# Attention and two gated feed-forward layers on one core: how heads and weights are loaded at the start, and which tiles hold layer 1's last sums

## The chip, the core and the metric

The kernel runs on one core of a Trainium2 chip. The metric is the device time in microseconds of one execution, the median of several. Engines are named as the profile names them: PE (TensorE matmul), PEld (its weight loads), DVE (VectorE), ACT (ScalarE), POOL (GpSimd), SP (SyncE, which here only issues DMAs).

## What is computed

Attention over 4 batches of 8 heads, sequence 576, head size 64, with a causal mask and a forget-gate bias made of running sums of `s`. The result, 2304 tokens by 512, goes through two feed-forward layers of width 2048, the first with a hard-swish gate, the second with Silu.

```
cum  = cumsum(maximum(s, 0)); bias = -(cum[:, None] - cum[None, :])
p    = softmax(where(causal, -1e9, q @ k.T / 8 + minimum(bias, 0)))
x    = concat_heads(p @ v)                      # 2304 x 512
h    = x @ w1_in;  x2 = (h * clip(h + 3, 0, 6) / 6) @ w1_out
h    = x2 @ w2_in; out = (h * sigmoid(h)) @ w2_out
```

The scale is a factor of `q`, `k` and `v` are float32, and the four weight matrices are float64 in memory.

## The kernel before

**Numbers.** Each product is three matmuls (high by high, low by high, high by low), so that operands are held in a high and a low part. A weight matrix is cut into 16 pieces, `i0` to `i15` of w_in and `o0` to `o15` of w_out, each a DMA of 512 KB of raw 32-bit word pairs. A piece of layer 1 is made usable by six operations after its load (class `Chunk`, line 147 on): ACT `fields` (L159, L160), DVE `join` (L168, L172, L175), ACT `high` (a cast at L120), DVE `low` (L186). That is four DVE operations a piece, 128 for the 32 pieces of layer 1. The class `Feed` steps all pieces through these stages, one stage of each of several pieces with every call of `tick`: three ticks at the start, then 0.4 a slot over the first nine slots, then 2 a slot.

**Stages.** Nine slots of attention heads alone come first, in which PE is kept from idling by small matmuls (`keep_clock`, L86). Then come slots that hold one head and one step of layer 1: `first` (the product with a w_in piece, L259 to L261), the gate (ACT L271, DVE L272), `second` (the product with a w_out piece, L298 to L300). A step needs the pieces `i` and `o` of its number. The steps run over two blocks of tokens in turn: block 0 with pieces 0 to 7, block 1 with pieces 0 to 7 two at a time, then block 0 and block 1 with pieces 8 to 15. The gates are counted here as g0 to g7 (block 0), g8 to g11 (block 1, pairs), g12 and on. Layer 2 starts where the last sums of layer 1 are complete, with matmuls at L1008 to L1010 and L1024 to L1026, a gate on ACT (L1066, L1067) and DVE (L1068).

**Order.** The tile framework's scheduler sets the order of each engine's instructions at build time from its own estimates of time; on the chip each engine runs its list in order, and an instruction that waits holds all that stand behind it in that list. So does a DMA that waits in SP's list.

**Start.** `s` is loaded, made non-negative and summed by one scan over 576 elements (L343, L346) into `crow`. Each of the first 14 heads has a tile of its own (`inA...`) with q and k of 64 rows, and two more rows of sums (L418, L419: DMAs out of `crow`) and of constants (L406, L407: memsets on POOL); v comes by a third DMA (L396). The tiles borrow the slots of pieces not loaded yet (`spare`). The first three raw weight loads (L147) stand in SP's list between the first two heads' loads and their rows of sums. `cum_d` is a copy of the sums in DRAM, out of which later heads take theirs.

**Border of the layers.** `finish1` (L698 on) takes the last block's sums out of PSUM into four tiles `o7_*` by ACT and DVE copies, in the slot `s4` of `w7pool` and in slots `mag` of the stage pool, which are those in which raw words become magnitudes (ACT L160). They are stored by L712 to `x2T_d` and read back. A first use of Silu at L1066 brings a load of ACT's function table. `outs2` asks for a tick of layer 2's w_out pieces in the last steps of layer 1 (L1127 on).

## Time and profile before

| | us |
|---|---|
| median of 3 runs | 1021.71 (1020.31 to 1023.79) |
| profiled execution, its own time | 1023.73 |
| span of its trace | 1021.6 |
| PE busy | 991.8 (97%) |
| DVE busy | 723.7 (71%) |
| ACT busy | 523.4 (51%) |
| POOL busy | 204.5 (20%) |

The page gives PE 97% of the span. Its 40 slices of 25.5 us show where the rest is: PE has 8, 8, 7, 8 tenths in the first four slices, 9 in all others but one (8, at 638 to 664 us) and the last (7). The granted clock is under full only in the first four slices. DMA moves 153 to 297 GB/s in those slices and 44 to 70 in the next five. The chain that ended last is 89% PE.

### The profile page before, as it was taken

What the parts mean: (1) busy time and instruction counts of PE and PEld (TensorE: products, weight loads), DVE (VectorE), ACT (ScalarE), POOL (GpSimd) and SP (SyncE); (2) the same over time, 40 slices, a digit from 0 to 9 for tenths busy, and PEclk for the clock granted to TensorE, in tenths of its full rate; (3) what the DMA queues carried; (4) which work ended last, traced back from release to release, by engine and by line L of the source; (5) the groups of instructions that cost most, each with busy time, mean ns of one, the idle gap of its engine ahead of it and who ended that gap; (6) DMA issues with size and microseconds to landing.
All of it is one profiled execution on the core that took longest, in us unless ns stands there. A gap on an engine that the chain in (4) does not pass through costs nothing.

```text
span 1021.6 us, 18386 instructions
## 1 busy us (share of the span) xinstructions
PE 991.8 (97%) x6404; PEld 914.1 (89%) x6404; DVE 723.7 (71%) x1788; ACT 523.4 (51%) x1143; POOL 204.5 (20%) x382
## 2 busy tenths in 40 slices
PE   8878999999999999999999999899999999999997
PEld 5777999999999999999998888789988899888996
DVE  6799987788778888887738896977574343743343
ACT  6688755554555665665516563755353232532232
POOL 5001133444344444444411221000000000000000
PEclk9989999999999999999999999999999999999999
DMA  4685122222312222222114956343354332433411
GB/s 153 209 297 182 44 61 70 61 64 56 93 51 73 78 71 71 78 72 70 58 43 145 373 224 226 120 178 132 127 187 162 136 140 77 173 135 115 144 72 63
DMA packets 52068, 124.80 MB, mean 122 GB/s; under 512 B 10004, under 2 KB 31752, under 8 KB 48648
## 3 DMA queue, kind: packets, MB, share of 16 engines
q1 hardware_dynamic: 51528, 122.97, 35.7%
q8 instruction: 51, 0.84, 0.3%
q10 hardware_dynamic: 448, 0.66, 0.2%
q14 instruction: 41, 0.34, 0.1%
HBM read 98.96 MB, written 24.63 MB: 121 GB/s over the span
## 4 chain that ended last, share of the span: by engine, by line
PE 89%; DVE 5%; DMA 2%; ACT 2%; POOL 1%; issue 1%; SPq 0%; DVEq 0%; ACTq 0%; POOLq 0%
PE ph L259 6%; PE ph L260 6%; PE acc L299 6%; PE ph L261 6%; PE acc L300 6%; PE acc L298 6%; PE a L1024 6%; PE a L1025 6%; PE a L1026 6%; PE h L1008 5%; PE h L1009 5%; PE h L1010 5%; PE poB L616 4%; PE pt0B L566 1%; PE pt1B L566 1%; PE poA L631 1%
## 5 line engine op out<-in xcount | busy, mean ns | idle before, releaser
L299 PE MATMUL acc<-gl,wo 128*128 128x256 f32 (+1 forms) x512 | 153.8, 301 | 2.8 <-DVE gl L279 2.8
L259 PE MATMUL ph<-xh,wi 128*128 128x256 f32 (+1 forms) x512 | 153.3, 300 | 0.3 <-DVE g L272 0.3
L300 PE MATMUL acc<-gh,wo 128*128 128x256 f32 (+1 forms) x512 | 152.5, 299 | 0.0
L260 PE MATMUL ph<-xl,wi 128*128 128x256 f32 (+1 forms) x512 | 152.4, 298 | 0.0
L261 PE MATMUL ph<-xh,wi 128*128 128x256 f32 (+1 forms) x512 | 151.9, 297 | 0.0
L298 PE MATMUL acc<-gh,wo 128*128 128x256 f32 (+1 forms) x512 | 146.5, 301 | 0.1
L1066 ACT ACTIVATE gh<-h 128x384 fp32r<-128x384 f32 x96 | 50.3, 524 | 180.7 <-DVE h L1074 180.3
L1024 PE MATMUL a<-wo,gh 128*128 128x512 f32 x288 | 113.8, 395 | 2.4 <-ACT gh L1066 2.4
L1025 PE MATMUL a<-wo,gh 128*128 128x512 f32 x288 | 113.7, 395 | 0.0
L299 PEld LDWEIGHTS acc<-gl,wo 128*128 128x128 f32 x512 | 97.5, 191 | 6.9 <-DVE gl L279 3.6
L259 PEld LDWEIGHTS ph<-xh,wi 128*128 128x128 f32 x512 | 98.0, 191 | 4.2 <-DVE g L272 0.8
L300 PEld LDWEIGHTS acc<-gh,wo 128*128 128x128 f32 x512 | 97.5, 190 | 3.7
L260 PEld LDWEIGHTS ph<-xl,wi 128*128 128x128 f32 x512 | 97.9, 191 | 2.9
L261 PEld LDWEIGHTS ph<-xh,wi 128*128 128x128 f32 x512 | 97.8, 191 | 2.9
L298 PEld LDWEIGHTS acc<-gh,wo 128*128 128x128 f32 x512 | 96.5, 190 | 4.2 <-DVE gh L122 0.3
L1026 PE MATMUL a<-wo,gl 128*128 128x512 f32 x288 | 89.6, 393 | 1.2 <-DVE gl L1068 1.2
L1068 DVE TENSOR_TENSOR gl<-h,gh 128x384 fp32r<-128x384 f32 x96 | 53.4, 556 | 40.7 <-ACT h L1067 38.8
L1074 DVE TENSOR_TENSOR h<-h,u 128x384 f32<-128x384 f32 x72 | 40.0, 556 | 54.0 <-PE h L1010 53.7
L271 ACT ACTIVATE g<-ph,half 128x512 f32<-128x512 f32 (+1 forms) x76 | 50.3, 664 | 54.1 <-PE ph L261 53.4
L114 POOL TENSOR_SCALAR gh<-g 128x512 fp32r<-128x512 f32 x68 | 50.1, 737 | 133.2 <-DVE g L272 125.5
L272 DVE SCALAR_TENSOR_TENSOR g<-g,ph 128x512 f32<-128x512 f32 (+1 forms) x76 | 49.7, 655 | 33.4 <-ACT g L271 33.1
L1008 PE MATMUL h<-x0t,w 128*128 128x384 f32 x192 | 65.3, 340 | 0.7 <-DVE u L1074 0.7
(231 smaller groups left out, 2552.9 us busy)
## 6 DMA issues: line engine op xcount, KB each, us to landing
w<-w_d SPq DMA_DIRECT2D x18, 1792.0 KB
w_d<-w SPq DMA_DIRECT2D x8, 1792.0 KB
k2B<-in_kT_dram SPq DMA_DIRECT2D x64, 144.0 KB
rawi<-in_w1i_dram SPq DMA_DIRECT2D x16, 512.0 KB
rawo<-in_w1o_dram SPq DMA_DIRECT2D x16, 512.0 KB
rawi<-in_w2i_dram SPq DMA_DIRECT2D x16, 512.0 KB
rawo<-in_w2o_dram SPq DMA_DIRECT2D x16, 512.0 KB
q2B<-in_qT_dram SPq DMA_DIRECT2D x64, 80.0 KB
```

Of the source, the lines that this page charges most:

```text
L259: nc.tensor.matmul(o, wih[:, cs], xh[c], start=c == 0, stop=False)
L260: nc.tensor.matmul(o, wih[:, cs], xl[c], start=False, stop=False)
L261: nc.tensor.matmul(o, wil[:, cs], xh[c], start=False, stop=c == NDC - 1)
L298: nc.tensor.matmul(a, woh[:, cs], gh[:, jj, :], start=b0, stop=False)
L299: nc.tensor.matmul(a, woh[:, cs], gl[:, jj, :], start=False, stop=False)
L300: nc.tensor.matmul(a, wol[:, cs], gh[:, jj, :], start=False, stop=b1)
L1008: nc.tensor.matmul(ps, w[:, 0, cs], xh[:, c, :], start=c == 0, stop=False)
L1009: nc.tensor.matmul(ps, w[:, 0, cs], xl[:, c, :], start=False, stop=False)
L1024: nc.tensor.matmul(accs[t], gh[:, k, cs], woh, start=b0, stop=False)
L1025: nc.tensor.matmul(accs[t], gh[:, k, cs], wol, start=False, stop=False)
L1026: nc.tensor.matmul(accs[t], gl[:, k, cs], woh, start=False, stop=b1)
L1068: nc.vector.tensor_tensor(out=gl[:, i, o], in0=g, in1=f32(gh[:, i, o]), op=ALU.subtract)
```

## The change

- `keep_clock` at the start issues 18 matmuls, before 34.
- The first 14 heads are loaded in pairs (`load_two`): q, k, v and the rows of sums of two heads are one DMA each, and the constants of two heads one memset each. For the first pair, k, v and the second head's rows of sums are issued from ACT's queue, and its rows come out of `crow`; all later heads take theirs from `cum_d`. Eleven slots are borrowed rather than fourteen.
- The scan of `s` is done in two parts, 256 and 320 elements.
- A raw weight load of layer 1 is preceded by a copy of one element by POOL into the tile it will fill. The source is the end of `crow` for the first three, and from the fifth piece on the joined word of the piece four before it. The load can therefore not be issued before that piece's `join`. The three first loads come after the rows of sums and the store of `cum_d`.
- `split_rows` comes one slot later, and its rows borrow other slots.
- In the last block `finish1` uses tiles of the weight pool (slots `i0`, `i1`, in which layer 2's pieces `i8`, `i9` will be loaded) in place of `s4` and `mag`.
- A Silu of one element (`warm`) is put ahead of the last block's steps.
- `outs2` asks for more ticks in the last steps of layer 1: `min(2u + 2, t - 1)` for `u = t - 8`, before `u + 1`.

```
@@ -88,7 +88,7 @@
     def heads_of(x):
         return x.bitcast(BF16).rearrange("p (n two) -> p n two", two=2)[:, :, 1]
 
-    keep_clock(34, busy[:, :512])
+    keep_clock(18, busy[:, :512])
 
     NZ = (NFULL - 1) * P
     cmask = cpool.tile([P, NZ + P], F32, tag="cmask", name="cmask")
...
@@ -138,13 +138,15 @@
             pool, tag = self.home
             return pool.tile(shape, dt, tag=tag, name=f"{name}{self.nm}")
 
-        def load(self):
+        def load(self, queue=nc.sync, after=None):
             if self.src.dtype == F32:
                 self.val = self.place([P, DM], F32, "raw")
-                nc.sync.dma_start(self.val, self.src)
+                queue.dma_start(self.val, self.src)
             else:
                 raw = self.place([P, 2 * DM], I32, "raw")
-                nc.sync.dma_start(raw, self.src.bitcast(I32))
+                if after is not None:
+                    pool_copy(f32(raw[:1, :1]), after)
+                queue.dma_start(raw, self.src.bitcast(I32))
                 words = raw.rearrange("p (n two) -> p n two", two=2)
                 self.words = words[:, :, 0], words[:, :, 1]
 
...
@@ -211,7 +213,9 @@
             if lo == "v":
                 self.ch[t - 2].low(lo)
             if self.t < n:
-                self.ch[self.t].load()
+                if self.ch[self.t].key[1] == 0 and self.t >= 4:
+                    after = self.ch[self.t - 4].val[:1, :1]
+                self.ch[self.t].load(queue, after)
             self.t += 1
 
 
...
@@ -337,13 +341,17 @@
 
 
     srow, crow = [
-        wpool.tile([BH, S], F32, tag=f"{kd}{NF // 2 - 1}", name=f"{kd}row") for kd in "io"
+        wpool.tile([BH, S], F32, tag=f"{kd}{NF - 2}", name=f"{kd}row") for kd in "io"
     ]
     nc.sync.dma_start(srow, s)
-    nc.vector.tensor_scalar(
-        out=srow, in0=srow, scalar1=0.0, scalar2=1.0 / SCALE, op0=ALU.max, op1=ALU.mult
-    )
-    nc.vector.tensor_tensor_scan(crow, srow, srow, 0.0, ALU.add, ALU.bypass)
+    for a, z in ((0, T1), (T1, S)):
+        sr, cr = srow[:, a:z], crow[:, a:z]
+        nc.vector.tensor_scalar(
+            out=sr, in0=sr, scalar1=0.0, scalar2=1.0 / SCALE, op0=ALU.max, op1=ALU.mult
+        )
+        nc.vector.tensor_tensor_scan(
+            cr, sr, sr, crow[:, a - 1 : a] if a else 0.0, ALU.add, ALU.bypass
+        )
 
     def split_rows():
 
...
@@ -352,7 +360,7 @@
 
         f = NF - 1
         hi, lo = row(f"i{f}", "cumh"), row(f"o{f}", "cuml")
-        one, neg = row(f"i{NF // 2 - 2}", "one"), row(f"o{NF // 2 - 2}", "neg")
+        one, neg = row(f"o{NF - 3}", "one"), row(f"i{NF - 2}", "neg")
         nc.gpsimd.memset(f32(one), 1.0)
         nc.gpsimd.memset(f32(neg), -1.0)
         nc.scalar.copy(hi, crow)
...
@@ -389,16 +397,35 @@
             b, h, nm, nk, nq = self.b, self.h, self.nm, self.nk, self.nq
             if self.at < 14:
 
-                t = wpool.tile([P, 2 * DM], F32, tag=spare[self.at], name=f"in{nm}")
-                self.q2, self.k2 = t[:, :nq], t[:, nq : nq + nk]
-                self.va = t[:, DM + nk :][:, : self.nkc * D].rearrange("p (c d) -> p c d", d=D)
-                self.load_qk()
-                nc.sync.dma_start(self.va, v1[b, h, :, : self.nkc, :])
+                i = self.at % 2
+                if i == 0:
+                    self.load_two()
+                self.q2, self.k2, self.va = [x[:, i] for x in two[self.at // 2]]
                 return
             tags = ("qs", "kl") if self.whole and self.slot else ("q2", "k2")
             self.q2 = apool.tile([P, nq], F32, tag=tags[0], name=f"q2{nm}")
             self.k2 = apool.tile([P, nk], F32, tag=tags[1], name=f"k2{nm}")
             self.load_qk()
+
+        def load_two(self):
+            b, h, nm, nk, kc = self.b, self.h, self.nm, self.nk, self.nkc
+            j = self.at // 2
+            qk = wpool.tile([P, 2, 2, nk], F32, tag=spare[3 * (j // 2) + 2 * (j % 2)], name=f"in{nm}")
+            if j % 2 == 0:
+                two["v"] = wpool.tile([P, 4, kc, D], F32, tag=spare[3 * (j // 2) + 1], name=f"inv{nm}")
+            va = two["v"][:, 2 * (j % 2) :][:, :2]
+            q2, k2 = qk[:, 0], qk[:, 1]
+            two[self.at // 2] = q2, k2, va
+            nc.gpsimd.memset(q2[D : D + 2], 1.0)
+            nc.gpsimd.memset(k2[D : D + 2], -1.0)
+            hs = slice(h, h + 2)
+            nc.sync.dma_start(q2[:D], qT[b, hs, :, :nk].rearrange("h d n -> d h n"))
+            (nc.sync if self.at else nc.scalar).dma_start(
+                k2[:D], kT[b, hs, :, :nk].rearrange("h d n -> d h n")
+            )
+            (nc.sync if self.at else nc.scalar).dma_start(
+                va, v1[b, hs, :, :kc, :].rearrange("h p c d -> p h c d")
+            )
 
         def load_qk(self):
             b, h, nk = self.b, self.h, self.nk
...
@@ -413,8 +440,21 @@
 
 
             nk, q0, bh = self.nk, self.q0, self.bh
+            if self.at < 14:
+                if self.at % 2 == 0:
+                    q2, k2, _ = two[self.at // 2]
+                    if self.at:
+                        rows = cum_d[bh : bh + 2, :nk].rearrange("(o h) n -> o h n", o=1)
+                        nc.sync.dma_start(k2[D : D + 1], rows)
+                        nc.sync.dma_start(q2[D + 1 : D + 2], rows)
+                    else:
+                        for i in range(2):
+                            queue = (nc.sync, nc.scalar)[i]
+                            queue.dma_start(k2[D : D + 1, i], crow[i : i + 1, :nk])
+                            queue.dma_start(q2[D + 1 : D + 2, i], crow[i : i + 1, :nk])
+                return
             if self.whole:
-                src = crow if self.at < 4 else cum_d
+                src = cum_d
                 nc.sync.dma_start(self.k2[D : D + 1, :], src[bh : bh + 1, :nk])
                 nc.sync.dma_start(self.q2[D + 1 : D + 2, :], src[bh : bh + 1, q0:nk])
                 return
...
@@ -698,8 +738,12 @@
         n = sizes[blk][1]
         per = 512 // n
         for i, c in enumerate(range(0, NDC, per)):
-            pool, tag = (gpool, "g") if blk < NB1 - 1 else (stage, "mag") if i else (w7pool, "s4")
-            o = pool.tile([P, per, n], F32, tag=tag, name=f"o{blk}_{c}")
+            if blk < NB1 - 1:
+                o = gpool.tile([P, per, n], F32, tag="g", name=f"o{blk}_{c}")
+            else:
+                if i % 2 == 0:
+                    both = wpool.tile([P, 2, n], F32, tag=f"i{i // 2}", name=f"o{blk}_{c}")
+                o = both[:, i % 2 :][:, :1, :]
             a = sums1.pop((blk, c))
             if (blk, c) in kept:
                 for k in range(per):
...
@@ -811,10 +855,11 @@
     loaded = 2
     for hd in heads[:loaded]:
         hd.load()
-    ticks(3)
     for hd in heads[:loaded]:
         hd.load_cum()
     nc.sync.dma_start(cum_d, crow)
+    for _ in range(3):
+        feed.tick(after=crow[:1, S - 1 :])
     heads[0].places()
     k = 0
     p1 = p2 = None
...
@@ -838,7 +883,7 @@
                 tk[i] = int(feed_at)
                 feed_at -= tk[i]
         slot(cur, p1, p2, nx, loads, has_step, tk)
-        if nslot == 2:
+        if nslot == 3:
             split_rows()
         p1, p2 = cur, p1
         nslot += 1
...
@@ -1109,6 +1154,8 @@
         c0.enter_context(tc.tile_pool(name="ps_acc2", bufs=2, space=PSUM, reuse_waits="tile"))
     ]
     z0 = step
+    warm = stage.tile([P, DM], I32, tag="mag", name="warm")
+    nc.scalar.activation(f32(warm)[:, :1], f32(xsplit[NB1 - 1][0][0][NDC - 1][:, T1 : T1 + 1]), AF.Silu)
     while step < len(flat):
         t = step - z0
         first(step, 0)
...
@@ -1127,7 +1174,7 @@
         second(step - 1, 1)
         step += 1
         if t >= NF // 2:
-            outs2(t - NF // 2 + 1)
+            outs2(min(2 * (t - NF // 2) + 2, t - 1))
     second(step - 1, 0)
     second(step - 1, 1)
     c0.close()
```

**Pace of the conversions.** Of the 128 DVE conversion operations of layer 1, the order has this many ahead of each gate's L272:

| ahead of | g0 | g1 | g4 | g7 | g8 | g11 | g13 |
|---|---|---|---|---|---|---|---|
| before | 24 | 29 | 54 | 82 | 99 | 120 | 128 |
| after | 50 | 59 | 80 | 102 | 111 | 128 | 128 |

Ahead of the first score reduction (L523 on `pb0A0_0`) there are 6 before and none after. Between it and g8 four more rows of L523 stand after than before.

**The start, in SP's list.** `inA0_0` and `inA0_1` are the first heads' tiles (after: `inA0_0` and `inA0_2` are those of the first two pairs), `orow` is the tile of the sums. Before:

```order
L396 DMA inA0_0_160<-in_v1_dram 128x128
L409 DMA inA0_1_166<-in_qT_dram 64x256
L410 DMA inA0_1_166<-in_kT_dram 64x256
L396 DMA inA0_1_166<-in_v1_dram 128x128
L147 DMA rawi0_0_172<-in_w1i_dram 128x1024
L147 DMA rawo0_0_174<-in_w1o_dram 128x1024
L147 DMA rawi0_1_176<-in_w1i_dram 128x1024
L418 DMA inA0_0_160<-orow_156 1x16x16
L419 DMA inA0_0_160<-orow_156 1x16x16
L418 DMA inA0_1_166<-orow_156 1x16x16
```

After:

```order
L422 DMA inA0_0_146<-in_qT_dram 64x2x256
L422 DMA inA0_2_178<-in_qT_dram 64x2x256
L454 DMA inA0_0_146<-orow_140 1x16x16
L453 DMA inA0_0_146<-orow_140 1x16x16
L860 DMA cum_d_119<-orow_140 32x576
L423 DMA inA0_2_178<-in_kT_dram 64x2x256
L426 DMA invA0_0_147<-in_v1_dram 128x2x128
L448 DMA inA0_2_178<-cum_d_119 1x2x256
L449 DMA inA0_2_178<-cum_d_119 1x2x256
L422 DMA inA0_4_239<-in_qT_dram 64x2x256
L149 DMA rawi0_0_158<-in_w1i_dram 128x1024
L149 DMA rawo0_0_161<-in_w1o_dram 128x1024
```

The three raw loads moved from ahead of the rows of sums to behind them, behind the store of `cum_d`, and behind two reads from it.

**Up to the first gate, in DVE's list.** The rows just ahead of g0 (L272 on `g0`), where `rawX`, `magX` and `wX` are a piece's tiles, with layer and number. Before:

```order
L523 ISA pb0A1_2_654,mxA1_2_653<-ps0A1_2_664,cmask_120 128x128
L523 ISA mxA1_2_653 128x1
L523 ISA pb1A1_2_655,mxA1_2_653<-ps1A1_2_667,cmask_120 128x256
L523 ISA mxA1_2_653 128x1
L544 RECIPROCAL sums1_129<-sums1_129 128x2
L186 TENSOR_TENSOR wo0_2_764<-mago0_2_673,wo0_2_764 128x512
L272 SCALAR_TENSOR_TENSOR g0_627<-g0_627,ph0_607 128x256
```

After:

```order
L583 TENSOR_SCALAR sums0_111<-sums0_111 128x2
L678 TENSOR_TENSOR xtA1_0_612<-poA1_1_700,sums1_113 128x2x64
L170 SCALAR_TENSOR_TENSOR rawo0_6_853<-rawo0_6_853 128x512
L188 TENSOR_TENSOR wi0_5_937<-magi0_5_846,wi0_5_937 128x512
L174 TENSOR_SCALAR magi0_6_939<-magi0_6_939 128x512
L584 RECIPROCAL sums0_111<-sums0_111 128x2
L276 SCALAR_TENSOR_TENSOR g0_584<-g0_584,ph0_564 128x256
```

The piece being converted there is number 2 before and numbers 5 and 6 after.

**The border, in ACT's list.** `p1_0_0` is the first copy that layer 2 makes; `gh20_0` is the first gate on Silu. Before:

```order
L1083 COPY p1_0_0_9296<-h2_1_9297 128x384
L160 ACTIVATE mago1_5_9375<-rawo1_5_9133 128x512
L160 ACTIVATE mago1_6_9386<-rawo1_6_9176 128x512
L160 ACTIVATE mago1_7_9397<-rawo1_7_9219 128x512
L120 CAST wo1_5_9395<-mago1_5_9375 128x512
L1066 ACT_TABLE_LOAD
L1066 ACTIVATE gh20_0_9294<-h11_0_0_9321 128x384
```

After:

```order
L1128 COPY p1_0_0_9329<-h2_1_9330 128x384
L161 ACTIVATE rawo1_15_9666<-rawo1_15_9666 128x512
L120 CAST wo1_10_9657<-mago1_10_9247 128x512
L120 CAST wo1_11_9812<-mago1_11_9648 128x512
L161 ACTIVATE rawi1_8_9668<-rawi1_8_9668 128x512
L162 ACTIVATE magi1_8_9672<-rawi1_8_9668 128x512
L120 CAST wo1_12_9821<-mago1_12_9659 128x512
L1111 ACTIVATE gh20_0_9327<-h11_0_0_9354 128x384
```

The table load is gone from ahead of the gate, and so are three magnitudes and a cast; three casts and the fields of `rawo1_15` and `rawi1_8` stand there now.

**The border, in SP's list.** The stores of the last sums and the loads behind them. Before:

```order
L712 DMA x2T_d_137<-o7_0_9233 128x512
L712 DMA x2T_d_137<-o7_2_9239 128x512
L712 DMA x2T_d_137<-o7_1_9236 128x512
L712 DMA x2T_d_137<-o7_3_9242 128x512
L147 DMA rawo1_15_9699<-in_w2o_dram 128x1024
```

After:

```order
L756 DMA x2T_d_121<-o7_0_9268 128x512
L149 DMA rawo1_15_9666<-in_w2o_dram 128x1024
L756 DMA x2T_d_121<-o7_2_9273 128x512
L756 DMA x2T_d_121<-o7_0_9268 128x512
L756 DMA x2T_d_121<-o7_2_9273 128x512
L149 DMA rawi1_8_9668<-in_w2i_dram 128x1024
L149 DMA rawi1_9_9670<-in_w2i_dram 128x1024
```

`rawi1_8` and `rawi1_9` go into slots that the `o7` tiles hold, so that they can't be issued before these stores have landed.

## Rows read from the trace of the kernel before

**Rows 1.** Busy time of each engine in five stretches: length, busy (count), clock, DMA share, GB/s

```profile
12.79:46.98 34.19, 29.96 (x197) 23.25 (x195) 24.93 (x101) 22.94 (x70) 1.25 (x5) 0.95 0.57 166
46.98:108.29 61.31, 50.07 (x331) 45.56 (x330) 59.16 (x173) 51.14 (x121) 4.43 (x14) 0.89 0.66 223
108.29:128.00 19.71, 19.08 (x162) 18.83 (x163) 19.47 (x52) 14.90 (x36) 2.68 (x5) 1.00 0.18 49
200.00:300.00 100.00, 100.00 (x847) 99.53 (x846) 81.11 (x243) 51.82 (x134) 37.97 (x71) 1.00 0.24 68
640.00:660.00 20.00, 16.55 (x69) 13.53 (x69) 19.64 (x40) 15.73 (x30) 0.00 (x0) 0.91 0.37 122
```

**Rows 2.** PE timeline at the start: start us, us, line, out<-in, count, idle before

```profile
1.45 8.99 PE L86 MATMUL idle<-busy 128*128 128x512 bf16 x34 [1.45 <-DVE half L101]
11.73 0.46 PE L504 MATMUL ps0A<-inA 66*128 66x128 f32 x2 [1.29 <-POOL inA L407]
```

**Rows 3.** GpSimd timeline at the start

```profile
3.63 1.15 POOL L96 TENSOR_SCALAR_AFFINE_SELECT cmask<-cmask 128x128 f32<-128x128 f32 x1
4.84 0.30 POOL L407 MEMSET inA<- 2x256 f32 x1
```

**Rows 4.** SP queue timeline at the start: issue time and length of DMA instructions

```profile
0.73 0.40 SPq L342 DMA_DIRECT2D irow<-in_s_dram  x1
...
8.24 0.59 SPq L419 DMA_DIRECT2D inA<-orow  x1
```

**Rows 5.** DVE timeline at the start

```profile
2.68 0.63 DVE L343 TENSOR_SCALAR irow<-irow 32x576 f32<-32x576 f32 x1 [1.28 <-DMA irow<-in_s_dram]
...
12.79 0.28 DVE L523 CUSTOM_DVE_ANT_0 pb0A<-ps0A,cmask 128x128 f32<-128x128 f32 x1
```

**Rows 6.** PE timeline at the border of the layers

```profile
631.68 0.34 PE L1008 MATMUL h<-x0b,w 128*128 128x384 f32 x1
...
640.37 0.50 PE L1024 MATMUL a<-wo,gh 128*128 128x512 f32 x1 [0.19 <-ACT gh L1066]
...
643.22 0.97 PE L1026 MATMUL a<-wo,gl 128*128 128x512 f32 x3 [1.20 <-DVE gl L1068]
646.25 0.79 PE L1024 MATMUL a<-wo,gh 128*128 128x512 f32 x1 [2.06 <-ACT gh L1066]
```

**Rows 7.** DVE timeline inside the stretch of conversions

```profile
50.30 0.69 DVE L168 SCALAR_TENSOR_TENSOR rawo<-rawo 128x512 int32<-128x512 int32 x1
50.90 0.42 DVE L172 TENSOR_SCALAR mago<-mago 128x512 int32<-128x512 int32 x1
51.24 0.41 DVE L272 SCALAR_TENSOR_TENSOR g<-g,ph 128x256 f32<-128x256 f32 x1
...
52.11 0.69 DVE L175 CUSTOM_DVE_ANT_0 mago<-rawo,mago 128x1024 uint16<-128x1024 uint16 x1
52.72 0.68 DVE L186 TENSOR_TENSOR wi<-magi,wi 128x512 fp32r<-128x512 f32 x1
53.32 0.42 DVE L523 CUSTOM_DVE_ANT_0 pb1A<-ps1A,cmask 128x256 f32<-128x256 f32 x1
```

**Rows 8.** SP and ACT timelines: an uncontended weight load issued, and its first ACT operation

```profile
619.74 0.33 SPq L147 DMA_DIRECT2D rawo<-in_w2o_dram  x1
623.10 0.66 ACT L159 ACTIVATE rawo<-rawo 128x512 int32<-128x512 uint32 x1 [0.80 <-DMA rawo<-in_w2o_dram]
```

**Rows 9.** Chain of waits, two stretches: start us, us, what

```profile
63.48 4.99 DMA rawo<-in_w1o_dram
...
631.84 3.98 DMA x2T_d<-o
```

**Rows 10.** ACT timeline, before and at the border of the layers

```profile
546.30 0.69 ACT L271 ACTIVATE g<-ph,half 128x512 f32<-128x512 f32 x1 [4.21 <-PE ph L261]
...
638.49 1.28 ACT L1066 ACT_TABLE_LOAD   x1
639.79 0.53 ACT L1066 ACTIVATE gh<-h 128x384 fp32r<-128x384 f32 x1
```

98 lines of the change are left out of this document (72 added, 26 removed).

## The prediction

> **What bounds the kernel now.** I read the busy times by stretch first, because the shares of the whole span hide what matters here [rows 1]. Cut at the first score reduction (12.79), g0 (46.98) and g8 (108.29), they show two kernels. From g8 on PE is the bound: busy 19.08 of 19.71 us in the next stretch, and all of 100 us further on. Before g8 it is DVE: 59.16 of 61.31 us between g0 and g8, while PE has 50.07 at a clock of 0.89. So up to g8 the time is DVE's work plus its idle time, and an edit that moves work on PE, ACT or SP counts only if DVE gets its inputs sooner or later. Then I read the start. PE does dummies until 10.44 and its first score starts at 11.73 [rows 2]. Its row puts the wait down to POOL's memset, but that ended at 5.14 [rows 3]; the last of the rows of sums is issued at 8.24 [rows 4], so it is those DMAs that PE waits for. DVE reduces that score at 12.79 [rows 5]. The third place is the border of the layers: of 640 to 660 us PE is busy 16.55 at 0.91 [rows 1], after three waits of 0.19, 1.20 and 2.06 us, 3.45 together, on ACT and DVE [rows 6]. The clock's share there is about 0.09 x 16.55 = 1.5 us.
>
> **The start: earlier by about 3.9 us.** Without the raw loads in front, what decides is POOL's list. Its affine mask starts at 3.63 and takes 1.15, the memset behind it starts at 4.84 and takes 0.30 for 256 elements [rows 3]. With 512 elements in each of the two memsets around it I estimate the end of the second at 5.4 us. The row of sums goes into partitions that this memset writes, so its DMA starts then. The price of such a small DMA lies between 1.95 us (the load of `s`: issued at 0.73, its reader starts at 2.68) [rows 4, 5] and 3.5 us (8.24 to 11.73, with the raw loads in the same engines) [rows 2, 4]. I take one a little over 2 us, since the raw loads are gone from there: first score at 7.8, and with the 1.06 us of before between score and reduction [rows 2, 5], DVE starts at 8.9. The 18 dummies (8.99 / 34 = 0.26 each) end near 6.2, which leaves PE a gap of 1.6 us where it now has 1.29, so I put the smaller `keep_clock` at nothing. The halved scan is hidden under the memsets likewise.
>
> **DVE up to g8: longer by about 10 us of work, shorter in idle time.** From 12.79 to 108.29 DVE is busy 24.93 + 59.16 = 84.1 us of 95.5, idle 11.4, of which 9.3 lie ahead of g0 and 2.15 behind it [rows 1]. The order puts 111 conversion operations ahead of g8 where 99 stood, and it no longer does 6 of them ahead of the first score: 18 more in this stretch. Start to start, L168 takes 0.60, L172 0.34, L175 0.61 and L186 0.60 [rows 7], 0.54 on average, so 18 x 0.54 = 9.7 us. Four more rows of score reduction are at most 4 x 0.28 [rows 5]; I take 0.6. The work is 84.1 + 9.7 + 0.6 = 94.4, and g8 falls at 8.9 + 94.4 + idle = 103.3 + idle. It is level with before at an idle time of 5.0 us.
>
> No row shows how much idle time the new order has. Its lower bound is the 2.15 us of before behind g0, where conversions already stand between all other work; its upper bound is the 11.4 us of before. I take 6.1: the 26 conversions put ahead of g0 stand in the part that was idle, and this part will look more like the stretch behind g0, whose row it is nearest to (2.15); but raw words can't come before the rows of sums, the store of `cum_d` and its reads are through, and the first reductions will still wait for PE and ACT, some 4 us. That gives g8 at 109.4, **+1.1 us**, with ends of -2.8 and +6.4.
>
> **The tie of the loads.** A raw load now waits for POOL's copy, which waits for the join four pieces back, and later loads and copies of both lists wait behind it: SP's reads for the next heads, POOL's memsets for them. The chain from such a join to the first operation of the new piece is the copy and the issue (some 0.5), the landing, and 0.6 of ACT. The landing takes 3.36 us with free DMA engines (619.74 to 623.10) [rows 8] and 4.99 in the loaded start [rows 9]. So the chain is 4.5 to 6.1 us. In the new order, between such a join and the first DVE operation of the piece four later, stand operations that I sum by their kinds to 4.9 to 6.6 us. At the nearer landing, 3.36 to 4, the tie costs nothing, for that DVE work covers it; at 4.99 the shorter ones lack up to 1.2 us. I take nothing, since the same tie spreads out the burst in which the 4.99 arose.
>
> **Behind g8.** Conversions that stood here have been done, 12 of the 29 left before. PE idles 0.63 us in this stretch [rows 1]; the rest of the work is unchanged. I take **-0.6 us** (ends -0.6 and 0).
>
> **The border.** All times here are from B = 631.68, layer 2's first matmul [rows 6]. The table load of 1.28 us [rows 10] leaves ACT's list ahead of the gate, and it goes where ACT idles over 4 us at a time (4.21 ahead of 546.30) [rows 10]; without that cover it would cost those 1.28. What is late next is not the table. The stores of the last sums take until about B + 4.1 (631.84 + 3.98) [rows 9]. Now `rawi1_8` waits in SP's list for them, is issued near B + 4.6 and lands 3.36 to 4.99 later, at B + 8.0 to 9.6. ACT's list has its fields, its magnitude and a cast (about 0.6 each, as the magnitudes and casts there) ahead of the first gate, which so starts at about B + 9.8, where it now starts at B + 8.1 (639.79) [rows 10]. PE, out of first products at B + 8.5, waits near 2 us where it waited 0.19. But its later waits shrink, as they wait for the same chain of ACT and DVE: the last one ended at B + 14.57 (646.25) [rows 6]. I put it at B + 15 to 15.7, so **+0.9 us**. Ends: -0.7, where the DMA lands at its best and the casts are taken in the gaps, and +2.5, with 4.99 us for it and the 5 us of conversions that the faster `outs2` puts on DVE there.
>
> The first gate on Silu starts 1.30 us after its table load does [rows 10], so the row shows no time behind the load. The Trainium skill ("ScalarE: Activation LUTs", section "What ACT_TABLE_LOAD costs") counts a drain of 1380 ns beside the 1283 ns, 2.66 us in all. By that the border would give back 1.38 us more and the sum below would be 0.0 instead of +1.4. The trace doesn't bear it out, and I go by the row.
>
> **The sum.** +1.1 - 0.6 + 0.9 = +1.4 us: 1025.1 against the profiled execution's own 1023.73 us (its span is 1021.6, the 2.1 around it don't change). The median of the runs is 2.0 lower, 1021.71, so **1023.1 us**. All ends at once give -4.1 and +8.9. A difference under 0.3%, 3.1 us, is about what a measurement of this kernel can't tell from no change.
>
> **Rivals.**
> Faster: the conversions really fill the idle time. DVE's idle falls to 2.15 us from the first reduction on, g8 comes 2.8 us earlier, -0.6 follows. At the border the new tiles free the raw slots and the three waits shrink to between none and all: -0.7 to -4.95 (3.45 + 1.5). That is -4.1 to -8.4, about -6: 1015.7 us. For it: the 9.3 idle us ahead of g0 are real, and conversions are the only work at hand that needs no PE. Against it: both must come out well, and ACT's list puts a late load ahead of the first gate.
> Slower: the tie is too short. It decides from the point where a landing takes over 4.1 us or so: then most of the first 28 pieces come late, 24 of them under the tie, in pairs, and DVE waits about 0.7 us for each pair, with SP's and POOL's lists held meanwhile. 12 x 0.7 = 8.4 us on top of my sum less what idle of 6.1 already holds (about 2): 1023.1 + 6.4 = 1029.5. For it: the 4.99 row, and DMA engines 0.66 busy from g0 to g8 [rows 1, 9]. Against it: fewer loads are out at a time.
> The change doesn't do what it says at the start: POOL or the pair's larger loads hold the first score at 11 us or later. The 3 us or so don't come off: 1026. For it: the loads of two heads are a burst too; against: they are less than the raw loads were.
>
> **How the numbers follow.** My sum, within 0.3% (1018.6 to 1024.8): 0.43. The faster rival: 0.27. The slower ones: 0.22 and 0.08. So faster 0.27, same 0.43, slower 0.30. The range leaves out about a tenth at each end: down to 1016.5, a little above the middle of the faster rival, up to 1029.0, near the slower one. The forecast's own range would be 1018.6 to 1024.8.
>
> **What would show it.** The first score at 7.8 us, the first reduction at 8.9, g8 (L272) at 109 and DVE's idle time between those two at 6 us: if idle is 2 to 3, the faster rival holds; if ACT's L159 shows waits on the raw DMA of a microsecond again and again, the slower. The first score at 11 would be the third. At the border, the first gate at B + 9.8, and PE's last wait ending at B + 15 to 15.7; an end before B + 13 proves me wrong there. Behind g8 PE should have no idle time left until the border.

## The result and the profile after

The changed kernel takes 1028.36 us (median of 6 runs, 1026.07 to 1031.27) where the kernel before takes 1021.75 beside it: a ratio of 1.0058 (1.0044 to 1.0073), or 5.9 us slower (4.5 to 7.5). That lies in the stated range, near its upper end, and not where the forecast was: the forecast was no change (+1.4 us), and it is a loss well above 0.3%. The profiled execution after is one of the faster ones, 1027.12 us with a span of 1025.3, against 1023.73 and 1021.6 before, so the two traces show only 3.4 of the 5.9 us. What one trace shows of a stretch varies from execution to execution by some us; that is why the experiments below are read by their runs, with several traces for each stretch.

The view by stretch, cut at the first score reduction, g0 and g8 as in [rows 1], then 100 us further on and the first 20 us from the first layer-2 product on; last, that stretch of the kernel before:

```profile
8.83:58.16 49.33, 40.27 (x216) 31.97 (x215) 42.95 (x152) 40.49 (x107) 9.46 (x26) 0.81 0.76 216
58.16:113.01 54.85, 45.50 (x314) 43.20 (x314) 50.21 (x146) 40.31 (x96) 9.04 (x28) 0.86 0.52 168
200.00:300.00 100.00, 100.00 (x843) 99.49 (x842) 80.27 (x246) 51.37 (x136) 41.14 (x73) 1.00 0.25 71
634.44:654.44 20.00, 15.87 (x75) 13.46 (x74) 17.80 (x36) 13.09 (x26) 0.00 (x0) 0.91 0.80 280
```

```profile
631.68:651.68 20.00, 16.55 (x76) 14.31 (x75) 17.18 (x35) 15.53 (x28) 0.00 (x0) 0.91 0.50 177
```

g8 falls at 113.01 where it fell at 108.29. DVE (third busy time in a row) has done 42.95 + 50.21 = 93.2 us of work by then and was idle for 11.0 us. The later stretches are PE's, as before. The granted clock (third figure from the end) is under full at the border too, 0.91 in both kernels, and not only in the first slices of the page. From g8 to the first layer-2 product it now takes 521.4 us (634.44 - 113.01), before 523.4; from there to the end of the span 390.9, before 389.9. So +4.7, -2.0 and +1.0 make the 3.7 us of the two spans.

The start, in PE's and DVE's timeline (answers to [rows 2, 5]):

```profile
1.45 5.78 PE L86 MATMUL idle<-busy 128*128 128x512 bf16 x18 [1.45 <-DVE half L101]
7.34 0.46 PE L544 MATMUL ps0A<-inA 66*128 66x128 f32 x2
```

```profile
8.83 0.27 DVE L563 CUSTOM_DVE_ANT_0 pb0A<-ps0A,cmask 128x128 f32<-128x128 f32 x1
```

The first score is at 7.34 instead of 11.73, its reduction at 8.83 instead of 12.79. The 18 dummies end at 7.23, so that PE has a gap of 0.1 us.

Then the tie. ACT's waits between g0 and g8, grouped by line and what they waited for, first after, then before:

```profile
ACT rawi L161 <- DMA rawi<-in_w1i_dram: 5.7, 4, 2.6
ACT g L275 <- PE ph L265: 5.1, 3, 3.1
ACT rawo L161 <- DMA rawo<-in_w1o_dram: 3.1, 3, 1.2
```

```profile
ACT g L271 <- PE ph L261: 5.0, 4, 2.1
ACT rawo L159 <- DMA rawo<-in_w1o_dram: 1.4, 1, 1.4
ACT rawi L159 <- DMA rawi<-in_w1i_dram: 0.5, 1, 0.5
```

ACT waits 8.8 us for raw words after and 1.9 before. The longest of these waits, in the timelines of DVE, POOL, SP and ACT after:

```profile
78.68 0.68 DVE L177 CUSTOM_DVE_ANT_0 magi<-rawi,magi 128x1024 uint16<-128x1024 uint16 x1
```

```profile
80.37 0.31 POOL L433 MEMSET q2A<- 2x256 f32 x1 [5.45 <-PE ps1A L544]
81.00 0.37 POOL L114 TENSOR_SCALAR rawi<-magi 1x1 f32<-1x1 f32 x1
```

```profile
80.85 0.56 SPq L437 DMA_DIRECT2D k2A<-in_kT_dram  x1
81.46 0.44 SPq L458 DMA_DIRECT2D k2A<-cum_d  x1
81.95 0.25 SPq L459 DMA_DIRECT2D q2A<-cum_d  x1
82.29 0.36 SPq L149 DMA_DIRECT2D rawi<-in_w1i_dram  x1
```

```profile
86.17 0.67 ACT L161 ACTIVATE rawi<-rawi 128x512 int32<-128x512 uint32 x1 [2.59 <-DMA rawi<-in_w1i_dram]
86.74 0.46 ACT L120 COPY th0A<-pt0A 128x384 f32<-128x384 f32 x1
```

The join of the piece four before is over at 79.36. POOL's copy of it (the gate of the load) stands in POOL's list behind two memsets for the next head, the first of which waited for PE until 80.37, and so starts at 81.00. It is over at 81.37; the load is issued only at 82.29, behind loads for that head in SP's list, and ACT's first operation on it starts 3.88 us after that. From the join's end to the issue that makes 2.93 us: 1.64 in POOL's list, 0.37 of copy, 0.92 in SP's. ACT stands for 2.59 us, and the copy of the transposed probabilities (L120 on `pt0A`), which needs no raw word at all, stands behind it.

The other waits are of two kinds. The next longest, 1.65 and 1.20 us ahead of ACT's operations at 103.67 and 110.58, also had their gates held: 4.37 and 4.15 us lie between the join's end and the issue. Those of 1.15 and 1.04 us, at 69.64 and 73.61, had not: 0.67 and 0.41 us from join to issue, and 3.63 and 3.79 from issue to ACT's operation. So of the 8.8 us, 5.4 stand behind gates that POOL's and SP's lists held back, and 2.2 behind loads that went out at once and were still late. (Of the last two, 0.92 us follows a load that took 5.52 us, and 0.27 one that took 3.73.)

The border (answers to [rows 6, 9, 10]): the chain of waits, ACT and PE after.

```profile
635.55 4.59 DMA x2T_d<-o
...
640.22 3.52 DMA rawi<-in_w2i_dram
```

```profile
643.76 0.66 ACT L161 ACTIVATE rawi<-rawi 128x512 int32<-128x512 uint32 x1 [3.25 <-DMA rawi<-in_w2i_dram]
644.32 0.66 ACT L162 ACTIVATE magi<-rawi 128x512 f32<-128x512 f32 x1
644.87 0.61 ACT L120 CAST wo<-mago 128x512 fp32r<-128x512 f32 x1
645.38 0.52 ACT L1111 ACTIVATE gh<-h 128x384 fp32r<-128x384 f32 x1
```

```profile
645.96 0.50 PE L1069 MATMUL a<-wo,gh 128*128 128x512 f32 x1 [3.02 <-ACT gh L1111]
650.90 0.50 PE L1069 MATMUL a<-wo,gh 128*128 128x512 f32 x1 [1.11 <-ACT gh L1111]
```

With B = 634.44, the load that waits for the stores is issued at B + 5.8 (the chain has the stores' 4.59 us start at B + 1.1; before, 3.98 us from B + 0.2), the first gate starts at B + 10.9 (before B + 8.1), and PE's last wait ends at B + 16.5 (before B + 14.6). PE's waits are 4.13 us together, before 3.45.

### The profile page after: what moved, and what is told of

It is laid out like the page before. It is cut to its first block, busy times and chain, and to the rows that moved or that the text cites. A ratio compares the mean times of both kernels' runs of the same rounds, so it can differ in the third digit from the quotient of the medians.

```text
span 1025.3 us, 18350 instructions
## 1 busy us (share of the span) xinstructions
PE 992.7 (97%) x6388; PEld 917.6 (89%) x6388; DVE 720.3 (70%) x1790; ACT 519.8 (51%) x1144; POOL 223.3 (22%) x399
## 4 chain that ended last, share of the span: by engine, by line
PE 84%; DMA 5%; DVE 5%; issue 1%; POOL 1%; ACT 1%; SPq 1%; POOLq 0%; ACTq 0%; DVEq 0%
PE ph L263 6%; PE acc L303 6%; PE acc L304 6%; PE ph L264 6%; PE ph L265 6%; PE acc L302 6%; PE a L1069 6%; PE a L1071 6%; PE a L1070 6%; PE h L1053 5%; PE h L1054 5%; PE h L1055 5%; PE poB L656 4%; DMA rawi<-in_w1i_dram 2%; PE pt0B L606 1%
## 5 line engine op out<-in xcount | busy, mean ns | idle before, releaser
L114 POOL TENSOR_SCALAR gh<-g 128x512 fp32r<-128x512 f32 x68 | 59.9, 882 | 130.4 <-DVE g L276 113.1
L1069 PEld LDWEIGHTS a<-wo,gh 128*128 128x128 f32 x288 | 54.2, 188 | 13.9 <-ACT gh L1111 5.6
```

The costliest lines, as they stand in the source:

```text
L114: nc.gpsimd.tensor_scalar(out=o, in0=i, scalar1=1.0, scalar2=1.0, op0=ALU.mult, op1=ALU.mult)
L1069: nc.tensor.matmul(accs[t], gh[:, k, cs], woh, start=b0, stop=False)
```

## The experiments

Three parts were taken apart: the **start** (loads of two heads, halved scan, first raw loads behind the rows of sums, 18 dummies, `split_rows` a slot later), the **tie** of later raw loads to a join, and the **border** (tiles of the last sums, early Silu, pace of layer 2's pieces). All ratios are against the kernel before, run beside each, with 95% intervals.

| kernel | ratio | g8 at | DVE idle to g8 | ACT waits for raw words, g0 to g8 | g8 to B | B to end |
|---|---|---|---|---|---|---|
| before | 1 | 108.3 | 11.4 | 1.9 | 523.4 | 389.9 |
| changed | 1.0058 (1.0044 to 1.0073) | 113.0 | 11.0 | 8.8 | 521.4 | 390.9 |
| start and tie | 1.0028 (1.0013 to 1.0044) | 116.7 | 13.0 | 11.4 | 522.1 | 387.8 |
| border alone | 1.0041 (1.0025 to 1.0056) | 106.3 | | | 523.2 | 392.9 |
| start and border | 1.0008 (0.9994 to 1.0023) | 112.0 | 7.9 | 1.3 | 520.5 | 392.3 |
| tie alone | 1.0027 (1.0010 to 1.0044) | 109.0 | 17.5 | 14.8 | 530.5 | 389.6 |
| start alone | 0.9979 (0.9966 to 0.9992) | 110.5 | 7.0 | 2.7 | 520.4 | 385.7 |
| start, tie to the fifth piece back | 1.0004 (0.9985 to 1.0023) | 111.6 | 10.7 | 4.6 | 523.6 | 388.3 |

DVE's idle time is the length of the two stretches less its busy time in them; the waits are summed over ACT's rows that by the profile end on a raw load; B is the first product at L1008 (or that line in the kernel at hand). All columns but the ratio are from one trace each, and traces of the same code differ: the four with the new start, no tie and the low part on DVE (those of the start with early Silu and of the tiles in i2 and i3, both below, beside the two here) have g8 at 108.0 to 112.0.

Where DVE idles tells more than g8. Ahead of g0 it idles 6.4 to 8.3 us in the three traces with the new start and a tie, 4.5 to 7.5 in those four without. From g0 to g8 it is 4.6 us (changed), 5.6 (start and tie) and 2.4 (fifth piece back) with the tie, 0 to 0.5 without it. Of the changed kernel's 4.6 us, 2.3 end on ACT's first operation on raw words and 1.3 on a gate of ACT's that waited for PE; of the 5.6 us, 3.8 end on ACT's first operation.

**Start and tie, without the border's edits.**

```
-            if blk < NB1 - 1:
...
-                    both = wpool.tile([P, 2, n], F32, tag=f"i{i // 2}", name=f"o{blk}_{c}")
+            pool, tag = (gpool, "g") if blk < NB1 - 1 else (stage, "mag") if i else (w7pool, "s4")
...
-    nc.scalar.activation(f32(warm)[:, :1], ..., AF.Silu)
...
-            outs2(min(2 * (t - NF // 2) + 2, t - 1))
+            outs2(t - NF // 2 + 1)
```

> The changed kernel with layer 1's last sums in their old tiles, without the early Silu and with the old pace of layer 2's pieces; start and tie as changed. Theory (the border costs about 1 us, as first layer-2 product to end takes 390.9 us after and 389.9 before): g8 stays at 113 us, and the stretch from the first layer-2 product to the end falls by 1.0 us; median about 1027.4. Rival (the new border gains, and all of the loss is in the start): that stretch grows, median 1029 or more.

1.0028, where the changed kernel has 1.0058: about 3 us come back, not 1. B to the end falls by 3.1 us (390.9 to 387.8). The border costs, and by the medians more than the two first traces showed (the difference of two such ratios is good to about 2 us); but half of the loss remains.

**The border's edits alone, on the kernel before.**

```
+                if i % 2 == 0:
+                    both = wpool.tile([P, 2, n], F32, tag=f"i{i // 2}", name=f"o{blk}_{c}")
+                o = both[:, i % 2 :][:, :1, :]
...
+    nc.scalar.activation(f32(warm)[:, :1], ..., AF.Silu)
...
-            outs2(t - NF // 2 + 1)
+            outs2(min(2 * (t - NF // 2) + 2, t - 1))
```

> The kernel before with the border's three edits alone. Theory: g8 at 108.3 as before, 1.0 us more from the first layer-2 product to the end; median about 1022.8. Rival (the late load ahead of the first gate costs more where the start is not late): 1024 or more. Rival (the border gains): 1020 or less.

1.0041, or 4.2 us: the first rival's number, not the theory's. Whether the border costs more here than with the new start (3.0 us) the intervals don't tell. Its chain of waits and PE's waits show why it can be more than after (same columns as above):

```profile
630.89 6.43 DMA x2T_d<-o
...
641.04 0.68 ACT rawi L159
```

```profile
643.26 0.80 PE L1028 MATMUL a<-wo,gh 128*128 128x512 f32 x1 [5.17 <-ACT gh L1070]
648.19 0.50 PE L1028 MATMUL a<-wo,gh 128*128 128x512 f32 x1 [0.86 <-ACT gh L1070]
```

By the chain the stores take 6.43 us, 4.59 in the trace after and 3.98 before. With B = 629.50 here, they start at B + 1.4, the load behind them is issued at B + 8.0 (637.45), ACT's first operation on `rawi1_8` comes at B + 11.5, and PE's last wait ends at B + 18.7.

**The changed kernel without the tie** (start and border).

```
-                if self.ch[self.t].key[1] == 0 and self.t >= 4:
-                    after = self.ch[self.t - 4].val[:1, :1]
```

> The changed kernel without the tie from the fifth piece on; the first three loads still come behind the rows of sums. In the order 114 conversions stand ahead of g8 where the changed kernel has 111. Theory (DVE's work ahead of g8 is what costs, 0.54 us a conversion): g8 at 113.0 + 1.6 = 114.6, median about 1030. Rival (the tie makes raw words late, and DVE's idle time of 11.0 us falls to 6 without it): g8 at 108 to 110, median about 1024.

1.0008: the tie costs about 5 us, and DVE's idle time falls from 11.0 to 7.9 us, most of the way to the 6 of the rival, though g8 comes only 1.0 us earlier in these two traces: DVE starts 0.4 us later, and with 3 more conversions ahead of g8 it is busy 94.9 us instead of 93.2. (This trace's own time lies 2.9 us over its kernel's median, that of the changed kernel 1.2 us under.) The theory, that only DVE's amount of work counts, falls.

**The tie alone, on the kernel before.**

```
+                if after is not None:
+                    pool_copy(f32(raw[:1, :1]), after)
...
+                if self.ch[self.t].key[1] == 0 and self.t >= 4:
+                    after = self.ch[self.t - 4].val[:1, :1]
```

> The kernel before with the tie alone. 89 conversions stand ahead of g8 where before has 99, 6 ahead of the first score as before. Theory (DVE's work): 10 x 0.54 = 5.4 us less up to g8, so g8 at 103 if idle time stays at 11.4; some of it is given back behind g8, where 10 more conversions stand; median 1017 to 1020. Rival (the tie makes raw words late): idle time grows by as much or more, g8 at 108 or later, median 1022 or more.

1.0027, the rival again: 10 conversions fewer ahead of g8, and yet 2.8 us slower. ACT waits 14.8 us for raw words between g0 and g8, DVE is idle for 17.5 us up to g8, and the stretch behind g8 is 7 us longer than before: the waits go on there, 5.0 us of ACT's for raw words in the next 62 us. (The traced execution lies 4.8 us over its kernel's median; how much of these waits the others have is not shown.) One of the waits ahead of g8, in ACT's timeline, with the last operation of a head's scores ahead of it and a cast behind it:

```profile
103.15 0.18 ACT L540 ACTIVATION_READ_ACCUMULATOR pb1A<-pb1A,mxA 128x1 f32 x1
107.05 0.68 ACT L161 ACTIVATE rawo<-rawo 128x512 int32<-128x512 uint32 x1 [3.71 <-DMA rawo<-in_w1o_dram]
107.63 0.60 ACT L120 CAST wi<-magi 128x512 fp32r<-128x512 f32 x1
```

**The start alone** (no tie, old border: the edits of the first and the third experiment together).

> The changed kernel without the tie from the fifth piece on and with the old border: what is left is the loads of two heads, the halved scan, the later first raw loads and the shorter dummies. Theory (parts add up: the tie and the border each cost 3 to 4 us, the start by itself gains): 3.4 us under before, as the kernel without the tie less the border's 4.2 us gives, so 0.996 to 0.998 of before; g8 near 112 as without the tie, PE without idle time behind it, and 389 us from the first layer-2 product to the end. Rival (the low clock of the start, 0.67 to 0.81, makes the start a loss by itself): 1.000 or more of before.

0.9979, 2.1 us faster (0.8 to 3.5). The expected value was 3.4; what holds is that the start by itself gains, against the rival: its granted clock is 0.71 and 0.90 in the two stretches to g8, where the changed kernel has 0.81 and 0.86. Its view by stretch, to g0 and to g8 and from there on to 163 us:

```profile
8.66:62.59 53.93, 42.81 (x213) 33.97 (x213) 46.94 (x155) 44.27 (x114) 4.32 (x13) 0.71 0.91 294
62.59:110.47 47.88, 43.21 (x319) 41.44 (x318) 47.88 (x145) 39.37 (x94) 4.34 (x13) 0.90 0.34 110
110.47:163.26 52.79, 52.79 (x457) 52.51 (x457) 38.92 (x106) 27.04 (x67) 14.39 (x22) 1.00 0.16 46
```

From g0 to g8 DVE is not idle at all (47.88 of 47.88), and behind g8 PE is not (52.79 of 52.79). g8 itself is 2.2 us later than before, and the stretch from g8 to B 3.0 us shorter. The other 4.2 us by which this trace is shorter than before's lie behind B, where nothing was changed: PE has the full clock there in the first 20 us (1.00, before 0.91) and waits once, for 2.06 us. What of that belongs to the start was not taken apart.

The parts add up. The tie costs 5.0 us by the start alone against start and tie (1.0028 - 0.9979), and 5.1 by the changed kernel against the same without the tie (1.0058 - 1.0008). The border costs 3.0 and 3.0 by the same sort of differences (1.0058 - 1.0028, 1.0008 - 0.9979), and each is good to about 2 us. That start -2.1, tie +5 and border +3 make 5.9 says nothing more, since the second and third are differences along the same way; what shows it is that each comes out the same with and without the other. On the kernel before, the tie costs 2.8 and the border 4.2 us.

**Which part of the border: only the tiles moved, to the slots i0 and i1.**

```
+                if i % 2 == 0:
+                    both = wpool.tile([P, 2, n], F32, tag=f"i{i // 2}", name=f"o{blk}_{c}")
+                o = both[:, i % 2 :][:, :1, :]
```

> The kernel before with only the last sums' tiles moved to the slots i0 and i1. Theory (the cost of the border is the raw load that waits for the stores and stands ahead of the first gate): all of the border's loss, +3 to +5 us, PE's first wait 3 to 5 us, and the gate after the fields of rawi1_8. Rival (the faster pace of layer 2's w_out pieces, which this kernel hasn't, makes the loss): within 1 us of before.

1.0056 (1.0041 to 1.0072), 5.7 us: the whole loss of the border and a little more (within the intervals of the border alone), without the faster pace and without the early Silu. The table load stands behind the late piece here, in ACT's timeline:

```profile
642.58 1.28 ACT L1070 ACT_TABLE_LOAD   x1
643.87 0.52 ACT L1070 ACTIVATE gh<-h 128x384 fp32r<-128x384 f32 x1
```

PE's first wait is 5.78 us.

**The border with the tiles in i2 and i3**, once on the kernel before, once with the start and without the tie.

```
-                    both = wpool.tile([P, 2, n], F32, tag=f"i{i // 2}", name=f"o{blk}_{c}")
+                    both = wpool.tile([P, 2, n], F32, tag=f"i{i // 2 + 2}", name=f"o{blk}_{c}")
```

> The kernel before with the border's three edits, but the last sums in the slots i2 and i3, which no later piece takes. Theory (late load): nothing waits for the stores but their readers, PE's two waits shrink under before's 3.45 us; 1020 to 1023 where before has 1023. Rival (pace, or the copies into other tiles): +3 to +4 as with i0 and i1.

> The changed kernel without the tie and with the last sums in i2 and i3. Theory: the start's gain and a border that costs nothing add up, 3 to 5 us under before (0.995 to 0.997), which beats both kernels. Rival (parts don't add up): 0.999 or more.

1.0086 (1.0071 to 1.0101) and 1.0084 (1.0069 to 1.0100): both expectations failed, and the reason is in the edit. No weight piece takes i2 and i3, but layer 2's operands do: its function `parts` puts the two halves of `b11`, the first part of x, into them.

```
            n0 = 2 + 2 * ["b11", "b22", "t2", "b21", "t3", "t1", "t4"].index(name)
...
                wpool.tile([P, 2, TH], F32R, tag=f"i{n0 + k}", name=f"x{k}{name}_{b}")
```

So the cast that writes the high half (`x0b`, L976) now waits for the stores, and PE's first product of layer 2 that reads it waits for the cast. The chain of waits, ACT's and PE's timeline of the first:

```profile
635.34 6.51 DMA x2T_d<-o
```

```profile
641.87 0.83 ACT L976 CAST x0b<-xr 128x768 fp32r<-128x768 f32 x1 [0.54 <-DMA x2T_d<-o]
```

```profile
642.76 0.69 PE L1012 MATMUL h<-x0b,w 128*128 128x384 f32 x1 [6.03 <-ACT x0b L976]
```

So these two don't tell whether the border could be had for nothing, with tiles in slots that are really free; that stays untested. They show once more that whatever takes a slot of the last sums waits for their stores, 6.5 us here, with PE behind it.

**The tie one piece further back**, with the old border.

```
-                if self.ch[self.t].key[1] == 0 and self.t >= 4:
-                    after = self.ch[self.t - 4].val[:1, :1]
+                if self.ch[self.t].key[1] == 0 and self.t >= 5:
+                    after = self.ch[self.t - 5].val[:1, :1]
```

> The changed kernel with the old border, and with the tie to the joined word of the piece five before instead of four. 109 conversions stand ahead of g8. Theory (the tie leaves a load less time than its landing of 3.6 to 3.9 us needs, so ACT waits for raw words with the heads' and the gates' work behind it): one piece more, about 2 us of DVE's work and as much of other work, covers most of it; ACT's waits on raw loads between g0 and g8 fall from about 8 to under 3 us, and the loss against the kernel without the tie (0.998 of before) from 4 to 5 us to 1 or 2: 0.998 to 1.000. Rival (the tie costs by what POOL's and SP's lists hold back, not by the landing): as with the tie at four, 1.002 to 1.004.

1.0004 (0.9985 to 1.0023), between the start alone and the tie to the fourth piece back (1.0028): by the medians the tie's cost falls from 5.0 to about 2.5 us with one piece more, though the intervals of the two ties overlap. ACT's waits that end on a raw load fall from 11.4 to 4.6 us, but that is not all that its first operations on raw words (L161) wait: four more waits of theirs, 4.3 us together, end by the profile on POOL's list, three on the memset of `q2A` and one on a gate copy. The longest:

```profile
81.45 0.69 ACT L161 ACTIVATE rawo<-rawo 128x512 int32<-128x512 uint32 x1 [1.95 <-POOL q2A L433]
```

So the fall is from 11.4 to 8.9 us, where under 3 was expected, and for the cost 1 to 2. The distance is part of the cost; the rival, what POOL's and SP's lists hold back, has its part too, as the trace of the changed kernel shows above (5.4 of 8.8 us there). How the 5.0 us divide between the two no run took apart.

**The early Silu**, on the start alone, and on the kernel before.

```
+    warm = stage.tile([P, DM], I32, tag="mag", name="warm")
+    nc.scalar.activation(f32(warm)[:, :1], f32(xsplit[NB1 - 1][0][0][NDC - 1][:, T1 : T1 + 1]), AF.Silu)
```

> The start alone (no tie, old border) with the early Silu. Theory (the table load of 1.28 us stands on the chain to the first gate of layer 2): PE's wait at the border falls by up to 1.28 us, 0.997 of before, 0 to 1.3 us under the start alone. Rival (another wait ends last there): as the start alone, 0.998.

> The kernel before with the early Silu alone. Theory (1.28 us leave the chain to the first gate of layer 2, and nothing else changes): PE's first wait at the border goes, its last wait ends 1 us or so earlier than 14.6 us behind the first layer-2 product; 0.998 to 1.000 of before. Rival (the gain with the two-head loads, 2.8 us by the medians, is all the Silu's): 0.997 or less.

0.9951 (0.9934 to 0.9969), which beats both kernels by 5 us and more; but on the kernel before the Silu gives nothing, 1.0011 (0.9997 to 1.0026). There the table load is gone from the border and PE's last wait still ends at B + 14.3 (647.53, B = 633.21), against B + 14.6 (the theory had 1 us or so less). PE's timeline of that kernel:

```profile
644.50 0.97 PE L1026 MATMUL a<-wo,gl 128*128 128x512 f32 x3 [1.32 <-DVE gl L1068]
647.53 0.79 PE L1024 MATMUL a<-wo,gh 128*128 128x512 f32 x1 [2.06 <-ACT gh L1066]
```

Only the first of the three waits is gone, and another ends last. So on the kernel before the first expectation's rival is right (another wait ends last), and the second's, that the gain is all the Silu's, is not. Why the medians of the start with and without the Silu lie 2.8 us apart stays open: the intervals of the two (0.9966 to 0.9992 and 0.9934 to 0.9969) just touch, and in the traces B to the end is not shorter with it (389.0 against 385.7, at a granted clock of 0.83 and 1.00 in the first 20 us), while g8, far ahead of the edit, is 2.4 us earlier. What is shown is that this version is faster than both.

**Less DVE work: the low part on POOL.** The start with the early Silu, but with layer 1's subtractions on POOL.

```
-    feed = Feed([(kd, 0, f) for f in range(NF) for kd in "io"], "a", "v")
+    feed = Feed([(kd, 0, f) for f in range(NF) for kd in "io"], "a", "p")
```

> As the run before it, with the last DVE operation of each of layer 1's pieces (the low part, 0.60 us) on POOL, which is busy 4.4 us of the 48 or so between g0 and g8. 90 conversions of DVE stand ahead of g8 where 114 stood. Theory (up to g8 DVE's work sets the time): 24 x 0.54 = 13 us less of it; g8 5 to 13 us earlier as PE and ACT allow, and half or more of it kept at the end: 0.985 to 0.993 of before. Rival (DVE is not what sets it, or POOL's slower operations and the shared work make the pieces late): g8 at 108 or later, 0.996 or more.

1.0062 (1.0043 to 1.0081): slower by 11 us than the kernel that it was made of (0.9951). Groups of DVE and POOL between 60 and 108 us (line, operation, tiles, count, busy us, mean ns), first DVE with the low part on DVE (the start alone), then DVE and POOL with it on POOL:

```profile
L170 DVE SCALAR_TENSOR_TENSOR rawo<-rawo 128x512 int32<-128x512 int32 x7 | 4.8, 688 | 0.0
L174 DVE TENSOR_SCALAR mago<-mago 128x512 int32<-128x512 int32 x7 | 3.0, 423 | 0.0
```

```profile
L170 DVE SCALAR_TENSOR_TENSOR rawo<-rawo 128x512 int32<-128x512 int32 x10 | 9.7, 974 | 0.0
L170 DVE SCALAR_TENSOR_TENSOR rawi<-rawi 128x512 int32<-128x512 int32 x9 | 6.1, 680 | 0.0
L174 DVE TENSOR_SCALAR mago<-mago 128x512 int32<-128x512 int32 x7 | 5.6, 797 | 0.0
```

```profile
L188 POOL TENSOR_TENSOR wi<-magi,wi 128x512 fp32r<-128x512 f32 x7 | 10.3, 1477 | 10.0 <-ACT wi L120 9.8
L188 POOL TENSOR_TENSOR wo<-mago,wo 128x512 fp32r<-128x512 f32 x6 | 7.9, 1320 | 7.5 <-ACT wo L120 7.5
```

Of the operations that stayed on DVE, those shown on the `o` pieces take 0.97 and 0.80 us on average instead of 0.69 and 0.42; the same operation on the `i` pieces, L170 on `rawi`, stays at 0.68. L170 on `rawo` at 71.56 took 1.57 us while POOL subtracted from 71.29 to 72.58, and 0.68 where POOL did not subtract (76.02); at 67.67 it took 0.68 too, and the subtraction beside it 1.96. DVE's work ahead of g8 didn't fall by 13 us but grew: 44.50 + 58.52 = 103.0 us against 94.0 of the kernel that it was made of (94.8 of the start alone). g8 is at 121.0. DVE is busy for 58.52 of 58.71 us from g0 to g8, so that DVE does set the pace, and the edit failed as a way to give it less work.

## Why the prediction was right and wrong

The time lies in the range, but not for the forecast's reasons: +1.4 us were added up, and +5.9 measured. The range held because it had been drawn out to the slower rival; that it held is in part luck.

**The start: right, but for the dummies.** First score 7.34 (7.8 was said), first reduction 8.83 (8.9), the gain of 3.9 us for DVE is 4.0. The 18 dummies were put at 0.26 us each, an end near 6.2 and a gap of 1.6 us ahead of the score; they took 0.32 and left 0.1. In the traces of start and tie, of start and border and of the start with the early Silu they took 6.96, 6.79 and 6.66 us, and the first score came as late as 8.24, 8.07 and 7.94, right behind them. So the smaller `keep_clock` is not nothing: what is left of it can still hold the first score by up to 0.9 us.

**DVE's work: right.** 93.2 us ahead of g8 (94.4 said). g8 = 8.83 + 93.2 + 11.0 = 113.0.

**DVE's idle time and the tie: the step that failed.** I took an idle time of 6.1 us and nothing for the tie. Without the tie the idle time is 4.9, 5.6, 7.0 and 7.9 us in four traces, so that my 6.1 was a fair value for the new order itself. With the tie it is 11.0 and 13.0. The zero for the tie is what was mis-sized: by the runs it costs 5 us. I compared the chain from a join to the next piece's first operation, 4.5 us at the nearer landing, with DVE's work in between, 4.9 to 6.6, and called it covered. Two things were missing. The copy and the issue are some 0.5 us (0.41 and 0.67) only where nothing stands ahead of them. Ahead of ACT's three longest waits it was 2.93, 4.37 and 4.15 us from the join's end to the issue, since the copy stood in POOL's list behind memsets that waited for PE, and the issue in SP's list behind loads for the heads. And the piece's first operation is not on DVE but on ACT, which has less work to do in that time (40.3 of 54.9 us busy, DVE 50.2), takes its list in order, and holds scores and gates behind it, so that DVE's cover doesn't help: the loads that went out at once cost ACT 1.0 to 1.2 us each all the same. I had named those queues and put no price on them.

**The slower rival: near in number, by another condition.** It gave 1029.5, and the time is 1028.36. But it was to decide from landings over 4.1 us, and six of the seven loads that ACT waits for here land within 3.4 to 3.9 us; one takes 5.5. The tie was too short at the usual landing already, for ACT, and where POOL's and SP's lists held the load back, up to 4.37 us had gone by before it was issued. And the border, which it didn't hold, is 3 us of the sum.

**Behind g8: right in direction.** -2.0 in the traces (-0.6 said, ends -0.6 and 0). But it is not the idle time that goes: over the 54 us or so behind g8 PE idles 0.48 us, where it idled 0.75 before, and 1.7 of the 2.0 us are busy time of PE. Without the tie PE idles nothing there, and the whole stretch to B is 2.6 to 3.0 us shorter than before in three traces. I had taken the rest of that stretch as unchanged; what shortens it wasn't taken apart.

**The border: right mechanism, size too small.** A late raw load ahead of the first gate was foreseen. I said issue at B + 4.6, first gate at B + 9.8, last wait at B + 15 to 15.7; measured are B + 5.8, B + 10.9, B + 16.5. The trace after shows +1.0 us to the end, as the +0.9 said, but by the runs the border costs 3.0 to 4.2, beyond my end of +2.5. The terms that were off are the stores' start and their landing. I took the start of before, B + 0.2, and the 3.98 us of before [rows 9]; after, they start at B + 1.1 and take 4.59, and in the kernels with the border alone and the tiles alone they start at B + 1.4 and B + 1.7 and take 6.43 and 5.91. From B to the end the four traces with these tiles take 390.9 to 393.3 us, the eight with the old border, with or without the early Silu, 385.7 to 389.9.

**The table load.** 1.28 us on the chain by its row, so I let 1.28 go. On the kernel before, its removal gave 1.0011: another wait ended last. The Trainium skill ("ScalarE: Activation LUTs", section "What ACT_TABLE_LOAD costs") counts a drain of some 1380 ns beside the load. The traces don't bear it out: with the tiles alone, where the load stands on the chain, the gate starts 1.29 us after the load does (642.58 to 643.87).

**The faster rival** had half a case: the conversions do fill the idle time, 4.9 to 7.9 us instead of 11.4, as long as the tie is away. But g8 came hardly earlier or later (108.0 to 112.0, before 108.3), since more work stood ahead of it.

## What to carry to other kernels

A load that is made to wait for work on another engine must be costed on every in-order list that it passes: the gate's engine, the queue that issues it, and above all the engine that consumes it, with all that stands behind that consumer. Cover on a third engine is no cover, and a gate copy is only as early as what stands ahead of it in its own engine's list. A tile in a slot that a later load wants turns the old contents' store into that load's start; at a border between stages, where PE has nothing else to do, it went straight into PE's waits here. The engine order and the list of all that takes the slot, operands as well as weights, show it before any run.
